# Seven rows normalised on GpSimd by adding the negated mean, with other planner margins and planner rules

## The chip, the cores and the metric

The kernel runs on one core of one Trainium2 chip. The metric is device time in microseconds (us), the median of the runs shown; lower is better. The core has five instruction streams that run side by side and wait for each other through semaphores: TensorE (PE, matmuls; PEld is its weight load), ScalarE (ACT), VectorE (DVE), GpSimd (POOL) and SyncE (SP, which only issues DMAs here). GpSimd issues DMAs too.

## What is computed

One token block of 2048 rows and 640 columns is normalised, and goes through an attention branch and a feed-forward branch, whose results are added to the input:

```
xn  = (x - mean(x)) / sqrt(var(x) + 1e-5)              # by row
q   = xn @ wq   (32 heads of 20);  k = xn @ wk;  v = xn @ wv   (one key/value head for all)
p   = softmax(q k^T / sqrt(20));   attn = (p v) @ wo
ffn = relu(xn @ w1 + b1)**2 @ w2 + b2
out = x + attn + ffn
```

All arrays are bf16, F is 1536. The scores are 32 heads x 2048 queries x 2048 keys.

## The kernel before: its stages and what orders them

**Tiles.** The rows are 16 tiles of 128 (`st` 0 to 15). Attention is 32 blocks: a block is 512 queries of four heads. In a block, each of 16 key tiles (`kt`, 128 keys) and each of the four heads is one score tile of 128 x 512: 2048 score tiles in all.

**Two ways to the exponential.** A score tile comes from one matmul, `ps<-qT,kT` (L426). 1396 of the 2048 tiles go to ACT, which evaluates exp on two PSUM banks at a time (L1007, 128x1024) into `PT`; PE then multiplies `PT` with the values `vx`. The other 652 tiles go in sets of four through an approximation: DVE turns the score into an integer that is read as a bf16 power of two (L1196, "D1"), then three more copies shifted by fixed steps are made on GpSimd (INT64_ADD, L1216) or DVE (L1218), and PE multiplies the copies with `vx` or the scaled `vxs`. Two copies of a set can first be added, either by a DMA that accumulates (issued on GpSimd, L1231, a "pair sum") or on DVE (L1236); that saves PE one multiplication per sum.

**Head of the kernel.** For every row tile: mean and variance (DVE `bn_stats`, L494 to L496; rows 2 and 4 on ACT, L489 and L490, which give the negated mean), 1/sqrt (rows 0 to 3 on ACT; the others on GpSimd as a power of -1/2, L505, "PW"), the normalisation "XN" at L507, five PE transposes (L618, "T"), a copy out of PSUM on DVE (L621, "TE"), and for each pair of rows the keys (L633). XN is `(x op mean) * rstd` in one `tensor_scalar`. Rows 7, 8, 9, 10, 11, 14 and 15 (`POOLXN`) do it on GpSimd, the others on DVE. `op` is subtract; rows 2 and 4, whose mean comes negated, use add. After the last XN, GpSimd loads another library ("LIB", L515), and only then can it run INT64_ADD.

**The planner.** The Python code that builds the kernel holds a list scheduler. Each operation has a planned duration, a priority and predecessors; latencies between engines stand in `LATS`; a DMA's planned landing is `lat`. The scheduler walks through a planned time and fixes, once and for all, the order of the instructions on each engine. On the chip each engine then runs its list strictly in that order and waits where a semaphore says so. Planned costs that matter here: XN on GpSimd 0.87, XN on DVE 0.36, PW 0.52, an INT64_ADD pass `PPASS` 1.015, the library 10.8. Margins: `DMARG` is added to the planned landing of DMAs of the softmax sums, `DMEND` takes its place for block 29 (the last that goes through those DMAs, `emit_norm`). `RULES` gives, for each 10 us of planned time ("stage"), weights and thresholds that decide which ready operation is taken first, when PE makes extra DVE tiles, when pair sums are made by DMA, and so on. `fill` matmuls (`ps<-kT,zeros`) are put where PE would idle in the head.

**End of a block and tail.** A block's sums go PSUM -> `OR` (DVE, L1075) -> DRAM -> `R` -> reciprocal (DVE, L1079) -> DRAM -> broadcast -> multiply (DVE, L1101, "CM"). Blocks 30 and 31 use transposes instead. In the tail PE multiplies the last quarter of the attention output with `wo`, DVE and ACT add and copy it, SP stores it.

Of the kernel before, what the change touches and what calls it, by code (L numbers as in the profile page):

```python
# [78 lines left out]
ADPL = 0.31  # L79
ADLEAD = 2.3  # L80
# [29 lines left out]
         11: {'BEHIND': 0.05, 'ADP': 5, 'ND': 1},  # L110
         12: {'BEHIND': 0.6, 'NOPEN': 4, 'JIT': 0.7},
         14: {'EVP': 0.3, 'DGAP': 1.5, 'DRATE': 0.95, 'BEHIND': 0.12, 'IDLE': 0.15, 'NOPEN': 3, 'EPS': 0.06, 'MRG': 2, 'M1': 0, 'ADP': 3.5, 'JIT': 0.7, 'PVA': 0.9, 'D1P': 0.3, 'SQP': 2, 'DQP': 0.5, 'KEEP': 2, 'ADDM': 0.6, 'ADPM': 2.4, 'KEEPM': 1, 'KEEPX': -1, 'DVL': 0.9, 'P2': 2},
         15: {'EVP': 0.3, 'DGAP': 1.5, 'DRATE': 0.95, 'BEHIND': 0.12, 'IDLE': 0.15, 'NOPEN': 3, 'EPS': 0.06, 'MRG': 2, 'M1': 0, 'ADP': 3.5, 'JIT': 1.3, 'PVA': 1.05, 'D1P': 0.3, 'SQP': 2, 'DQP': 0.5, 'KEEP': 2, 'ADDM': 0.6, 'ADPM': 2.4, 'KEEPM': 1, 'KEEPX': -1, 'DVL': 0.9, 'P2': 2},
         16: {'BEHIND': 0.05, 'IDLE': 0.15, 'EPS': 0.12, 'MRG': 1, 'JIT': 0.9, 'R3': 2, 'ND': 1, 'ADPM': 2.4},
         17: {'BEHIND': 0.05, 'IDLE': 0.15, 'EPS': 0.12, 'MRG': 1, 'JIT': 0.9, 'R3': 2, 'ND': 1, 'ADPM': 2.4},
         18: {'DGAP': 1.5, 'EPS': 0.06},
         19: {'EPS': 0.12},
         20: {'IDLE': 0.15, 'PP': 0.9},
         21: {'EVP': 1.1, 'IDLE': 0.15, 'JIT': 0.8, 'D1P': 0.5, 'PP': 0.9},
         22: {'EVP': 0.3, 'MPRIO': 0.9, 'DGAP': 0.8, 'DLAST': 6, 'DRATE': 0.95, 'BEHIND': 0.12, 'IDLE': 0.3, 'EPS': 0.06, 'MRG': 1, 'M1T': 1.2, 'JIT': 0.8, 'PVA': 0.9, 'ND': 1, 'KEEP': 0, 'KEEPM': 2, 'KEEPX': -1, 'DVL': 99},  # L120
# [26 lines left out]
         50: {'DVL': 0.9},
         51: {'EVP': 0.3, 'DVL': 0.9},
         52: {'EVP': 0.3, 'M1': 1, 'PVA': 0.9, 'DVL': 0.9},
         53: {'EPS': 0.03, 'JIT': 1.3, 'P2': 1},  # L150
         54: {'EVP': 0.8, 'DRATE': 0.95, 'URG': 4, 'M1T': 0, 'ADP': 3.5, 'JIT': 0.7, 'PVA': 0.9, 'D1P': 0.5, 'SQP': 3, 'ND': 2, 'KEEPM': 2},
         55: {'EVP': 0.8, 'DRATE': 0.95, 'URG': 9, 'EPS': 0.03, 'M1T': 0, 'ADP': 3.5, 'JIT': 0.7, 'PVA': 0.9, 'D1P': 0.5, 'SQP': 3, 'ND': 2, 'KEEPM': 2},
# [1493 lines left out]
```

## Time and profile before

| what | us |
|---|---|
| median of 3 runs (lowest, highest) | 678.58 (677.88, 679.56) |
| the profiled execution's own time | 677.92 |
| its span, first to last instruction | 676.1 |
| busy: PE / ACT / DVE / POOL | 663.3 / 653.1 / 606.6 / 588.3 |

The profile is one execution recorded by the hardware. "Busy" is the time in which an engine had an instruction in flight; the rest of the span it waited. The profile's other views are: windows (busy time of every engine in a stretch), waits (who waited for whom, total us, times, longest), the timeline of one engine (start, us, instruction; in brackets the idle time before it and what ended it), the instructions of one line (duration minimum/median/maximum in ns) and the chain that ended last.

### The profile page before, as it was taken

What the parts mean: (1) busy time and instruction counts of PE and PEld (TensorE: products, weight loads), DVE (VectorE), ACT (ScalarE), POOL (GpSimd) and SP (SyncE); (2) the same over time, 40 slices, a digit from 0 to 9 for tenths busy, and PEclk for the clock granted to TensorE, in tenths of its full rate; (3) what the DMA queues carried; (4) which work ended last, traced back from release to release, by engine and by line L of the source; (5) the groups of instructions that cost most, each with busy time, mean ns of one, the idle gap of its engine ahead of it and who ended that gap; (6) DMA issues with size and microseconds to landing.
All of it is one profiled execution on the core that took longest, in us unless ns stands there. A gap on an engine that the chain in (4) does not pass through costs nothing.

```text
span 676.1 us, 22515 instructions
## 1 busy us (share of the span) xinstructions
PE 663.3 (98%) x9617; PEld 212.5 (31%) x9618; DVE 606.6 (90%) x1069; ACT 653.1 (97%) x723; POOL 588.3 (87%) x591
## 2 busy tenths in 40 slices
PE   8789999999999999999999999999999999999998
PEld 4342222333332222233333322222333333222454
DVE  8669999999999999999999999999999999998654
ACT  7689999999999999999999999999999999999996
POOL 1947999999999989999999999999998999999331
PEclk9799999999999999999999999999999999999999
DMA  9496856686887755767786689575799878775744
GB/s 316 139 205 192 187 124 123 140 169 136 178 176 148 149 114 116 151 128 156 149 163 143 127 170 193 104 140 118 143 186 191 165 152 160 137 141 106 164 100 108
DMA packets 55278, 103.18 MB, mean 153 GB/s; under 512 B 17026, under 2 KB 33170, under 8 KB 55114
## 3 DMA queue, kind: packets, MB, share of 16 engines
q0 software_dynamic: 19088, 69.74, 55.3%
q1 hardware_dynamic: 35514, 31.63, 16.3%
q8 instruction: 75, 1.23, 0.7%
q10 hardware_dynamic: 576, 0.38, 0.2%
q14 instruction: 25, 0.20, 0.1%
HBM read 22.81 MB, written 9.69 MB: 48 GB/s over the span
## 4 chain that ended last, share of the span: by engine, by line
PE 57%; ACT 32%; POOL 4%; DMA 3%; DVE 2%; SPq 1%; issue 0%
PE ps L426 55%; ACT PT L1007 32%; POOL big L507 2%; DMA tmore<-tmore 1%; DMA tmore<-x_sb 1%; POOL tmore L1216 1%; POOL x_sb L1216 1%; PE ps L589 1%; SPq L1090 1%; SPq L1088 1%; DVE tmore L1196 1%; POOL rstd L505 0%; PE ps L618 0%; DVE big L507 0%; DMA R<-drs 0%
## 5 line engine op out<-in xcount | busy, mean ns | idle before, releaser
L1007 ACT ACTIVATE PT<-ps 128x1024 bf16<-128x1024 f32 x700 | 644.1, 1085 | 12.2 <-PE ps L426 11.5
L1196 DVE TENSOR_SCALAR tmore<-ps 128x512 uint16<-128x512 f32 x652 | 421.9, 684 | 32.6 <-PE ps L426 24.9
L1216 POOL INT64_ADD tmore<-tmore x217 | 240.6, 1200 | 38.0 <-DVE tmore L1196 18.6
L426 PE MATMUL ps<-qT,kT 20*128 20x512 bf16 x2048 | 265.0, 385 | 1.6 <-DVE tmore L1196 0.8
L1216 POOL INT64_ADD x_sb<-tmore x221 | 245.4, 1208 | 12.3 <-PE ps L426 3.4
L426 PEld LDWEIGHTS ps<-qT,kT 20*128 20x128 bf16 x2048 | 66.6, 91 | 255.0 <-ACT PT L1007 219.5
L426 PE MATMUL ps<-PT,vx 128*32 128x512 bf16 x1396 | 132.9, 388 | 0.0
L426 PE MATMUL ps<-xnT,w_sb 128*32 128x512 bf16 x960 | 77.5, 383 | 0.1
L426 PE MATMUL ps<-w_sb,big 128*32 128x320 bf16 x1536 | 74.7, 301 | 0.0
L1231 POOL DMA_DIRECT2D tmore<-tmore x63 | 64.6, 1035 | 3.0 <-POOL tmore L1216 3.0
L1231 POOL DMA_DIRECT2D x_sb<-tmore x61 | 65.1, 1074 | 2.1 <-POOL x_sb L1216 1.8
L426 PE MATMUL ps<-tmore,vxs 128*32 128x512 bf16 x636 | 57.5, 383 | 1.2 <-POOL tmore L1216 0.7
L426 PE MATMUL ps<-x_sb,vxs 128*32 128x512 bf16 x632 | 56.8, 383 | 0.1
L426 PEld LDWEIGHTS ps<-PT,vx 128*32 128x32 bf16 x1396 | 33.6, 93 | 63.3 <-issue 56.0
L426 PE MATMUL ps<-tmore,vx 128*32 128x512 bf16 x492 | 46.6, 382 | 0.0
L426 PEld LDWEIGHTS ps<-w_sb,big 128*32 128x32 bf16 x1536 | 34.0, 96 | 27.0 <-issue 17.7
L737 DVE TENSOR_SCALAR hT_tmp<-ps,b1col 128x512 bf16<-128x512 f32 x48 | 35.7, 744 | 3.2 <-PE ps L426 2.6
L426 PE MATMUL ps<-xnT,wq_sb 128*32 128x512 bf16 (+2 forms) x480 | 33.7, 356 | 0.0
L426 PE MATMUL ps<-x_sb,vx 128*32 128x512 bf16 x324 | 31.7, 383 | 0.0
L426 PE MATMUL ps<-wo_c,OC 128*32 128x320 bf16 x608 | 30.6, 301 | 0.0
L426 PEld LDWEIGHTS ps<-xnT,w_sb 128*32 128x32 bf16 x960 | 18.8, 95 | 24.9 <-issue 18.8
L745 DVE TENSOR_TENSOR big<-hT_tmp 128x512 bf16<-128x512 bf16 x48 | 24.8, 526 | 0.1
(95 smaller groups left out, 328.8 us busy)
## 6 DMA issues: line engine op xcount, KB each, us to landing
tmore<-tmore POOLq DMA_DIRECT2D x63, 512.0 KB, 5.4
x_sb<-tmore POOLq DMA_DIRECT2D x61, 512.0 KB, 5.5
w_sb<-in_B_w_dram SPq DMA_DIRECT2D x8, 480.0 KB, 10.1
big<-OR SPq DMA_DIRECT2D x71, 40.0 KB
big<-drs SPq DMA_DIRECT2D x71, 40.0 KB
xb<-in_A_x_dram SPq DMA_DIRECT2D x1, 2560.0 KB, 11.7
xb<-b2r POOLq DMA_DIRECT2D x1, 2560.0 KB, 18.7
xr<-xb SPq DMA_DIRECT2D x16, 160.0 KB, 3.9
```

The source lines that it names most:

```text
L426: return lambda e: e.matmul(out_, l, r, start=start, stop=stop, tile_position=tp, skip_group_check=loose)
L507: xn_op[st] = op(f"XN{st}", eng, dur, lambda e: e.tensor_scalar(out=xn_sb[:, st, :], in0=x_sb[:, st, :], scalar1=mv[:, st, 0:1], scalar2=r ...
L589: return [lambda e: e.matmul(ps[:, PVB, :], ones_bf[:, :], hT_tmp[:, 0, :], start=True, stop=True)]
L737: o = Op(f"RL{qc}_{f}", "DVE", 0.66, [lambda e: e.tensor_scalar(out=hT_tmp[:, k % 2, :], in0=ps[:, bk, :], scalar1=b1col[:, f:f + 1], scal ...
L745: q = op(f"SQ{qc}_{f}", "DVE", 0.34, lambda e: e.tensor_tensor(out=h2T[:, f, :], in0=hT_tmp[:, k % 2, :], in1=hT_tmp[:, k % 2, :], op=ALU. ...
L1007: return Op(f"ACT{st_['j']}", "ACT", ACB + ACM * n, [lambda e: e.activation(out=PT[:, s0:s0 + n, :], in_=ps[:, b0:b0 + (n - 1) * db + 1:db ...
L1088: dd = op(f"OM{b}_{j}", "SP", 0.76, lambda e, p0=p0, n=n, sl=sl, j=j, o0=o0: e.dma_start(cbuf(2 * sl)[p0:p0 + n, :], OR[32 * j + o0:32 * j ...
L1090: bc = op(f"BC{b}_{j}", "SP", 0.40, lambda e, p0=p0, n=n, sl=sl, j=j: e.dma_start(cbuf(2 * sl + 1)[p0:p0 + n, :], drs[b, 1][512 * j:512 * ...
L1196: d1 = op(f"D1_{n}_{i}", "DVE", 0.60, lambda e: e.tensor_scalar(out=L[:, cs].bitcast(U16), in0=ps[:, bank, :], scalar1=XA, scalar2=XB, op0 ...
L1216: fn = lambda e, T=T, j=j: e.int64_add(out=T.bitcast(I64), in0=L.bitcast(I64), in1=TSTEP * j * 0x0001000100010001)
L1231: p = op(f"AD{a}_{n}", "POOL", ADDUR, lambda e, src=src, dst=dst: e.dma_start(dst, src, accum_op=ALU.add), dp + [ad_last.get(k)], dma=adse ...
```

## The change

In the statistics of a row, rows in `POOLXN` get one more DVE operation "NM" that multiplies the mean by -1 in place, and their XN uses add. The planner adds `ADM` (0.5) to the planned landing of a pair sum where the instruction that waits for it is neither on PE nor itself a pair sum. `DMEND` goes from 1.0 to 2.5. `RULES` is replaced as a whole: other values in nearly every stage, some stages left to the defaults. Nothing else in the code changes.

```diff
-DMEND = 1.0
+DMEND = 2.5
...
+ADM = 0.5
...
 RULES = {0: {'WARM': 1},
-         1: {'EVP': 0.3, 'PBIAS': 5, 'DGAP': 1.5, 'DRATE': 0.95, 'BEHIND': 0.12, 'IDLE': 0.15, 'NOPEN': 3, 'EPS': 0.06, 'MRG': 1, 'M1': 0, 'ADP': 3.5, 'JIT': 0.7, 'PVA': 0.9, 'D1P': 0.3, 'PP': 4, 'SQP': 2, 'DQP': 0.5, 'KEEP': 2, 'ADDM': 1.5, 'ADPM': 2.4, 'KEEPM': 1, 'KEEPX': -1, 'DVL': 0.9, 'P2': 2, 'WARM': 1},
...
+         1: {'EVP': 0.3, 'DGAP': 0.8, 'DLAST': 6, 'DRATE': 0.95, 'BEHIND': 0.12, 'IDLE': 0.3, 'URG': 2, 'EPS': 0.06, 'MRG': 1, 'M1T': 1.2, 'JIT': 0.8, 'PVA': 0.9, 'ND': 2, 'KEEP': 0, 'KEEPM': 2, 'KEEPX': -1, 'DVL': 99, 'WARM': 1},
...
-            t = max(t, d.fin + (d.lat if d.lat is not None else ADPL if self.add and d.eng == "POOL" else LATS.get((d.eng, self.eng), 0.1)))
+            t = max(t, d.fin + (d.lat + (ADM if d.add and not self.add and self.eng != "PE" else 0.0) if d.lat is not None else ADPL if self.add and d.eng == "POOL" else LATS.get((d.eng, self.eng), 0.1)))
...
                 opm = ALU.subtract
+                if st in POOLXN:
+                    s1 = op(f"NM{st}", "DVE", 0.08, lambda e: e.tensor_scalar(out=mv[:, st, 0:1], in0=mv[:, st, 0:1], scalar1=-1.0, scalar2=None, op0=ALU.mult), [ag], prio=p - 0.1)
+                    opm = ALU.add
```

What the two built programs hold, counted in their instruction lists:

| instructions | before | after |
|---|---|---|
| ACT exp: pairs / singles / triples of tiles | 696 / 4 / 0 | 693 / 1 / 3 |
| score tiles on ACT / on DVE | 1396 / 652 | 1396 / 652 |
| INT64_ADD passes on POOL / passes on DVE | 438 / 51 | 437 / 52 |
| pair sums by DMA / on DVE | 128 / 3 | 133 / 0 |
| multiplications with the copies (`vx`, `vxs`) on PE | 2084 | 2076 |
| fill matmuls `ps<-kT,zeros` | 60 | 44 |
| NM on DVE | 0 | 7 |
| GpSimd's list up to the library load (PW, XN, one DMA) | same order | same order |

Beyond the head, the interleaving of the same kinds of work differs almost everywhere on PE, DVE and POOL. Near the end, the multiply "CM" of block 29 stands after block 30's transposes in DVE's list, where it stood before it.

More of the change, by code (lines that the diff above doesn't have):

```diff
@@ L110 @@
[L110 to L120, printed above, removed]
@@ L147 @@
[L147 to L152, printed above, removed]
-         56: {'DGAP': 0, 'DRATE': 0.95, 'IDLE': 0.15, 'URG': 6, 'ADP': 2, 'R3': 3, 'D1P': 0.3, 'PP': 0.9, 'KEEP': 0, 'ADPM': 2.4, 'DVL': 2.4},
@@ new lines @@
+         5: {'EVP': 0.3, 'DGAP': 0.8, 'DLAST': 6, 'DRATE': 0.95, 'BEHIND': 0.12, 'URG': 2, 'EPS': 0.06, 'MRG': 1, 'M1T': 1.2, 'JIT': 0.8, 'PVA': 0.9, 'ND': 2, 'KEEP': 0, 'ADDM': 0.6, 'ADPM': 3.5, 'KEEPM': 2, 'KEEPX': -1, 'DVL': 99, 'WARM': 1},
+         6: {'DRATE': 0.95, 'IDLE': 0.15, 'URG': 4, 'ADP': 2, 'D1P': 0.3, 'PP': 4, 'SQP': 0.7, 'KEEP': 0, 'ADPM': 2.4, 'DVL': 2.4},
+         7: {'EPS': 0.12, 'MRG': 1, 'R3': 2},
+         8: {'EVP': 0.3, 'DGAP': 0.8, 'DLAST': 6, 'DRATE': 0.95, 'BEHIND': 0.12, 'IDLE': 0.3, 'URG': 3, 'NOPEN': 4, 'EPS': 0.06, 'MRG': 1, 'M1T': 1.2, 'JIT': 0.8, 'PVA': 0.9, 'ND': 2, 'KEEPM': 2, 'KEEPX': -1, 'DVL': 99},
@@ new lines @@
+         10: {'EVP': 0.3, 'DGAP': 0.8, 'DLAST': 6, 'DRATE': 0.95, 'BEHIND': 0.12, 'IDLE': 0.15, 'URG': 2, 'EPS': 0.06, 'MRG': 1, 'M1T': 1.2, 'JIT': 0.8, 'PVA': 0.9, 'PVD': 0.9, 'ND': 2, 'KEEP': 0, 'ADDM': 0.7, 'KEEPM': 2, 'KEEPX': -1, 'DVL': 99},
+         11: {'EVP': 0.3, 'DGAP': 0.8, 'DLAST': 6, 'DRATE': 0.95, 'IDLE': 0.15, 'URG': 2, 'EPS': 0.06, 'MRG': 1, 'M1T': 1.2, 'JIT': 0.8, 'PVA': 0.9, 'PVD': 0.9, 'ND': 2, 'KEEP': 0, 'ADDM': 0.9, 'KEEPM': 2, 'KEEPX': -1, 'DVL': 99},
+         12: {'EPS': 0.12, 'MRG': 1, 'JIT': 0.9, 'R3': 2, 'PVA': 0.9},
@@ new lines @@
+         13: {'EVP': 0.8, 'DGAP': 0.8, 'DLAST': 6, 'DRATE': 0.95, 'BEHIND': 0.12, 'IDLE': 0.3, 'EPS': 0.06, 'MRG': 1, 'M1T': 1.2, 'JIT': 0.8, 'PVA': 1.05, 'ND': 2, 'KEEP': 0, 'KEEPM': 2, 'KEEPX': -1, 'DVL': 0.9},
+         14: {'EVP': 0.3, 'DGAP': 0.8, 'DLAST': 6, 'DRATE': 0.95, 'BEHIND': 0.12, 'IDLE': 0.3, 'EPS': 0.06, 'MRG': 1, 'M1T': 1.2, 'JIT': 0.8, 'PVA': 0.9, 'ND': 2, 'KEEP': 0, 'KEEPM': 2, 'KEEPX': -1, 'DVL': 99},
+         15: {'EVP': 0.8, 'DRATE': 0.95, 'IDLE': 0.15, 'URG': 4, 'M1T': 1.2, 'ADP': 3.5, 'JIT': 0.7, 'PVA': 0.9, 'D1P': 0.5, 'SQP': 3, 'ND': 2, 'KEEPM': 2, 'KEEPX': 1},
@@ new lines @@
+         17: {'DGAP': 1.5, 'JIT': 0.9, 'ADDM': 0.5},
+         18: {'DGAP': 0.8, 'DLAST': 2, 'NOPEN': 4, 'JIT': 0.7, 'D1P': 0.5, 'ND': 1, 'KEEP': 0, 'KEEPM': 1},
+         19: {'EPS': 0.06, 'M1T': 0, 'D1P': 0.5},
+         20: {'MPRIO': 0.3, 'ADDM': 1.2, 'P2': 1},
+         21: {'MPRIO': 0.3, 'MRG': 9, 'ADDB': 0, 'JIT': 1.1, 'ADDM': 1.2, 'P2': 1},
+         22: {'EVP': 0.3, 'DGAP': 1.5, 'DRATE': 0.95, 'BEHIND': 0.12, 'IDLE': 0.15, 'NOPEN': 3, 'EPS': 0.03, 'MRG': 1, 'M1': 0, 'ADP': 3.5, 'JIT': 0.8, 'PVA': 0.9, 'D1P': 0.3, 'PP': 4, 'SQP': 2, 'DQP': 0.5, 'KEEP': 2, 'ADDM': 0.6, 'ADPM': 2.4, 'KEEPM': 1, 'KEEPX': -1, 'DVL': 0.9, 'P2': 2},
@@ new lines @@
+         23: {'DLAST': 2, 'MRG': 2, 'PVA': 1, 'KEEP': 3},
+         24: {'EVP': 0.3, 'DGAP': 0.8, 'DLAST': 6, 'DRATE': 0.95, 'BEHIND': 0.12, 'IDLE': 0.15, 'URG': 2, 'EPS': 0.06, 'MRG': 1, 'M1T': 1.2, 'JIT': 0.8, 'PVA': 0.9, 'PVD': 0.9, 'ND': 2, 'KEEP': 0, 'ADDM': 0.7, 'KEEPM': 2, 'KEEPX': -1, 'DVL': 99},
+         25: {'DRATE': 0.8, 'SQP': 3},
+         26: {'EVP': 0.8, 'DGAP': 0.8, 'DLAST': 6, 'DRATE': 0.95, 'BEHIND': 0.12, 'IDLE': 0.3, 'EPS': 0.06, 'MRG': 1, 'M1T': 1.2, 'JIT': 0.8, 'PVA': 1.05, 'ND': 2, 'KEEP': 0, 'KEEPM': 2, 'KEEPX': -1, 'DVL': 0.9},
@@ new lines @@
+         28: {'MPRIO': 0.3, 'PVA': 1.05, 'ADDM': 1.2, 'P2': 1},
+         30: {'PBIAS': 8, 'NOPEN': 3},
+         31: {'PBIAS': 8, 'NOPEN': 3},
+         32: {'EVP': 0.3, 'DGAP': 0.8, 'DLAST': 6, 'DRATE': 0.95, 'BEHIND': 0.12, 'IDLE': 0.3, 'EPS': 0.06, 'MRG': 1, 'M1T': 1.2, 'JIT': 0.8, 'PVA': 0.9, 'ND': 2, 'KEEP': 0, 'ADDM': 1.5, 'KEEPX': -1, 'DVL': 99},
+         33: {'PBIAS': 8, 'M1T': 1.2},
+         34: {'EVP': 0.3, 'DGAP': 0.8, 'DLAST': 6, 'DRATE': 0.8, 'BEHIND': 0.12, 'IDLE': 0.3, 'EPS': 0.03, 'MRG': 1, 'M1T': 1.2, 'ADP': 5, 'JIT': 0.8, 'R3': 2, 'PVA': 0.9, 'PVD': 1.5, 'D1P': 3, 'KEEP': 0, 'ADDM': 0.3, 'KEEPM': 2, 'KEEPX': 0, 'DVL': 99},
@@ new lines @@
+         35: {'EPS': 0.03, 'KEEP': 2},
+         36: {'EPS': 0.03, 'PVA': 0.8, 'KEEP': 2},
+         37: {'DLAST': 2, 'EPS': 0.03, 'PVA': 0.8, 'PP': 0.9, 'KEEP': 2, 'DVL': 99},
+         38: {'M1T': 0.6, 'D1P': 0.5},
+         39: {'EVP': 0.8, 'PBIAS': 8, 'DRATE': 0.95, 'URG': 9, 'M1T': 1.2, 'ADP': 3.5, 'JIT': 0.8, 'PVA': 1, 'ND': 2, 'KEEPM': 0, 'KEEPX': 1},
+         40: {'EVP': 0.8, 'PBIAS': 8, 'MPRIO': 0.3, 'DGAP': 0.8, 'DLAST': 6, 'DRATE': 0.95, 'BEHIND': 0.12, 'IDLE': 0.3, 'NOPEN': 4, 'EPS': 0.06, 'MRG': 2, 'M1T': 1.2, 'JIT': 1.1, 'PVA': 0.8, 'PVD': 1.2, 'DQP': 1.5, 'ND': 1, 'KEEPM': 2, 'KEEPX': -1, 'DVL': 99},
@@ new lines @@
+         41: {'EVP': 0.8, 'PBIAS': 8, 'MPRIO': 0.5, 'DRATE': 0.95, 'IDLE': 0.6, 'URG': 4, 'M1T': 1.2, 'ADP': 3.5, 'JIT': 1.1, 'PVA': 0.9, 'D1P': 0.5, 'SQP': 3, 'ND': 2, 'KEEPX': 1},
+         43: {'DGAP': 0.3, 'IDLE': 0.3, 'URG': 4, 'R3': 3, 'QKP': 0, 'ND': 1, 'KEEPX': 2},
+         44: {'URG': 6, 'EPS': 0.12, 'MRG': 1, 'R3': 2},
+         45: {'IDLE': 0.3, 'URG': 4, 'PVA': 0.8, 'PVD': 1.2, 'PP': 4, 'ND': 1, 'ADDM': 0, 'KEEPX': 2},
+         46: {'NOPEN': 4, 'EPS': 0.12, 'D1P': 1},
+         47: {'DGAP': 0.3, 'IDLE': 0.3, 'URG': 4, 'QKP': 0, 'ND': 1, 'KEEPX': 2},
@@ new lines @@
+         48: {'PBIAS': 8, 'DGAP': 0.3, 'IDLE': 0.3, 'URG': 4, 'DQP': 1.5, 'QKP': 0, 'ND': 1, 'KEEPX': 2},
+         49: {'IDLE': 0.15, 'URG': 4, 'DQP': 3, 'ND': 1, 'KEEPX': 2, 'P2': 1},
+         50: {'EVP': 0.3, 'PBIAS': 5, 'MPRIO': 0.9, 'DGAP': 1.5, 'DRATE': 0.95, 'BEHIND': 0.12, 'IDLE': 0.15, 'NOPEN': 3, 'EPS': 0.06, 'MRG': 1, 'M1': 0, 'ADP': 3.5, 'JIT': 0.7, 'R3': 1, 'PVA': 0.9, 'D1P': 0.3, 'SQP': 2, 'DQP': 3, 'KEEP': 0, 'ADDM': 1, 'ADPM': 2.4, 'KEEPM': 1, 'KEEPX': 0, 'DVL': 0.9, 'P2': 2},
@@ new lines @@
+         51: {'EVP': 0.3, 'PBIAS': 5, 'MPRIO': 0.9, 'DGAP': 0.5, 'DRATE': 0.95, 'BEHIND': 0.12, 'IDLE': 0.15, 'NOPEN': 3, 'EPS': 0.06, 'MRG': 1, 'M1': 0, 'M1T': 0.9, 'ADP': 3.5, 'JIT': 0.7, 'R3': 1, 'PVA': 0.9, 'D1P': 0.3, 'SQP': 2, 'DQP': 3, 'KEEP': 0, 'ADDM': 1, 'ADPM': 2.4, 'KEEPM': 1, 'KEEPX': 0, 'DVL': 0.9, 'P2': 2},
+         52: {'EVP': 1.1, 'URG': 3, 'EPS': 0.06},
+         53: {'DRATE': 0.95, 'NOPEN': 3, 'MRG': 1, 'D1P': 0.3},
+         54: {'EVP': 0.8, 'DGAP': 0.8, 'DLAST': 6, 'DRATE': 0.95, 'BEHIND': 0.12, 'IDLE': 0.3, 'EPS': 0.06, 'MRG': 1, 'M1T': 1.2, 'JIT': 0.8, 'PVA': 1.05, 'ND': 2, 'KEEP': 0, 'KEEPM': 2, 'KEEPX': -1, 'DVL': 0.9},
@@ new lines @@
+         55: {'PBIAS': 8, 'EPS': 0.12, 'MRG': 1, 'R3': 2},
+         56: {'MPRIO': 0.3, 'ADDM': 1.2, 'P2': 1},
+         57: {'MPRIO': 0.3, 'ND': 1, 'ADDM': 1.2, 'P2': 1},
+         58: {'MPRIO': 0.3, 'ND': 1, 'ADDM': 1.2, 'P2': 1},
+         59: {'EVP': 0.8, 'PBIAS': 8, 'DRATE': 0.95, 'URG': 9, 'M1T': 1.2, 'ADP': 3.5, 'JIT': 0.8, 'PVA': 1, 'QKP': 0, 'ND': 2, 'KEEPM': 0, 'KEEPX': 1},
+         60: {'EVP': 0.8, 'PBIAS': 8, 'DRATE': 0.95, 'URG': 9, 'EPS': 0.06, 'M1T': 1.2, 'ADP': 3.5, 'JIT': 0.8, 'PVA': 1, 'ND': 2, 'KEEPM': 0, 'KEEPX': 1, 'DVL': 1.8},
@@ new lines @@
+         61: {'PBIAS': 8, 'NOPEN': 3, 'M1T': 0.6},
+         62: {'EVP': 0.3, 'DGAP': 1.5, 'DRATE': 0.95, 'BEHIND': 0.12, 'IDLE': 0.15, 'NOPEN': 3, 'EPS': 0.06, 'MRG': 0, 'M1': 0, 'ADP': 3.5, 'JIT': 0.7, 'PVA': 0.9, 'D1P': 0.3, 'PP': 0.9, 'SQP': 2, 'DQP': 0.5, 'QKP': 0, 'KEEP': 2, 'ADPM': 2.4, 'KEEPM': 1, 'KEEPX': -1, 'DVL': 0.9, 'P2': 2},
+         63: {'EVP': 0.3, 'MPRIO': 1.2, 'DGAP': 1.5, 'DRATE': 0.95, 'BEHIND': 0.12, 'IDLE': 0.15, 'NOPEN': 3, 'EPS': 0.06, 'MRG': 0, 'M1': 0, 'ADP': 3.5, 'JIT': 0.7, 'PVA': 0.9, 'D1P': 0.3, 'PP': 0.9, 'SQP': 2, 'DQP': 0.5, 'QKP': 0, 'KEEP': 2, 'ADPM': 2.4, 'KEEPM': 1, 'KEEPX': -1, 'DVL': 0.9, 'P2': 1},
@@ L164 @@
+         64: {'DGAP': 0.5, 'IDLE': 0.3, 'URG': 4, 'NOPEN': 1, 'MRG': 0, 'ADDN': 0.2, 'QKP': 0, 'ND': 1, 'KEEPM': 0, 'KEEPX': 2, 'DVL': 0.9},
+         65: {'DGAP': 0.8, 'IDLE': 0.3, 'URG': 4, 'NOPEN': 1, 'MRG': 0, 'ADDN': 0.2, 'R3': 1, 'QKP': 0, 'ND': 1, 'KEEP': 0, 'KEEPM': 0, 'KEEPX': 2, 'DVL': 0.9},
+         66: {'DGAP': 0.8, 'IDLE': 0.3, 'URG': 4, 'NOPEN': 1, 'MRG': 0, 'ADDN': 0.2, 'R3': 1, 'QKP': 0, 'ND': 1, 'KEEP': 0, 'KEEPM': 0, 'KEEPX': 2, 'DVL': 0.9}}
 HOOK = None
```

48 lines of the change are left out of this document (3 added, 45 removed).

## The prediction

> **What bounds the kernel now.** I read the windows first: which engine never rests, and where.
>
> ```profile
> 11.77:47.79 36.02, 30.43 (x474) 14.44 (x474) 25.00 (x78) 26.37 (x28) 25.86 (x20) 0.91 0.77 210
> ...
> sum 400.00, PE 399.34 PEld 117.16 DVE 377.57 ACT 400.00 POOL 386.49; mean PE 99.83 PEld 29.29 DVE 94.39 ACT 100.00 POOL 96.62
> ```
>
> The first row is the head, from the first exp to the keys of the last rows (length, then busy PE, PEld, DVE, ACT, POOL; granted clock; DMA). The second sums four windows from 100 to 500 us. There ACT is busy all 400 us. PE shows 99.83%, but it waits for ACT, as the waits of the whole span say, and so does its weight load:
>
> ```profile
> PEld ps L426 <- ACT PT L1007: 223.6, 574, 0.5
> ...
> ACT PT L1007 <- PE ps L426: 11.5, 11, 3.1
> ```
>
> So the score tiles on ACT set the pace from about 50 us on: 437 exps took 401.2 us there, 0.918 each.
>
> ```profile
> L1007 ACT ACTIVATE PT<-ps 128x1024 bf16<-128x1024 f32 x437 | 401.2, 1106 | 0.0
> ```
>
> The chain that ended last says 57% PE and 32% ACT; between engines that feed each other without a gap it may follow either, so I don't read a bound from it. The time to be won is ACT's idle time. ACT's waits, first for 11.77 to 75 us, then for 75 to 668 us, and its timeline, say where it lies:
>
> ```profile
> ACT PT L1007 <- PE ps L426: 9.8, 8, 3.1
> ```
> ```profile
> ACT PT L1007 <- PE ps L426: 1.7, 3, 1.2
> ```
> ```profile
> 21.30 5.09 ACT L1007 ACTIVATE PT<-ps 128x1024 bf16<-128x1024 f32 x5 [1.40 <-PE ps L426]
> 29.46 1.94 ACT L1007 ACTIVATE PT<-ps 128x1024 bf16<-128x1024 f32 x2 [3.07 <-PE ps L426]
> 32.82 1.02 ACT L1007 ACTIVATE PT<-ps 128x1024 bf16<-128x1024 f32 x1 [1.43 <-PE ps L426]
> ...
> 44.67 12.02 ACT L1007 ACTIVATE PT<-ps 128x1024 bf16<-128x1024 f32 x13 [3.12 <-PE ps L426]
> ```
>
> Four gaps, 1.40 + 3.07 + 1.43 + 3.12 = 9.0 us of the 9.8. What did PE and DVE wait for there?
>
> ```profile
> PE ps L618 <- POOL big L507: 5.2, 4, 1.8
> ...
> DVE xnT L621 <- PE ps L618: 6.3, 7, 2.0
> ```
> ```profile
> L507 DVE TENSOR_SCALAR big<-x_sb,mv,rstd x9: 433/440/668, 7.1 to 36.2; 128x640 bf16<-128x640 bf16 x9
> L507 POOL TENSOR_SCALAR big<-x_sb,mv,rstd x7: 2501/2504/2528, 17.9 to 40.9; 128x640 bf16<-128x640 bf16 x7
> ```
> ```profile
> L505 POOL TENSOR_TENSOR rstd<-mv,nhalf x12: 547/558/687, 12.1 to 40.3; 128x1 f32<-128x1 f32 x12
> ```
>
> PE waits for XN on GpSimd before its transposes, DVE for the transposes, ACT for PE. XN takes 2.50 us there, always. A row on GpSimd costs 0.56 (PW) + 2.50 + 0.08 in gaps = 3.14 us, and a new key tile gives ACT four score tiles, two exps, 2 x 0.918 = 1.84 us. While rows come every 3.14 us, ACT starves.
>
> **The change part by part.** *XN with add.* Seven instructions. The trace shows no such add on GpSimd, so I bound it: not below 0.56 (PW on one element), not above 2.50 (the subtract), since nothing in the form is larger. Between them lies a rate that GpSimd does show:
>
> ```profile
> 54.13 5.09 POOL L1216 INT64_ADD tmore<-tmore  x5 [10.68 <-DVE OR L1075]
> ```
>
> 1.02 us for 512 elements of 64 bits, 2.0 ns each, would make 640 elements 1.28 us. The planner carries 0.87 for XN on GpSimd; its other costs stand within 0.04 of their rows (PW 0.52 against 0.56, a pass 1.015 against 1.02), only XN is off by three. Whether 0.87 was once right for an add is not shown. I take 0.9, from between the pass's rate and PW, and keep both ends. What decides is whether a row falls below ACT's 1.84 us: the add must cost less than 1.84 - 0.56 - 0.08 = 1.20. At 0.9 it does; at 1.28 five consecutive rows (7 to 11) lose 5 x 0.08 = 0.4 us; at 2.50 nothing is won.
>
> The subtract alone is 2.50 us for 640 elements, 3.9 ns each. [...]
>
> *What is late next in the head.* With XN short, the head's 36.02 us window cannot shrink below its busiest engine: ACT 26.37, DVE 25.00 plus seven NMs, nearest row the 152 ns of the epsilon add:
>
> ```profile
> L499 DVE TENSOR_SCALAR mv<-mv 128x1 f32<-128x1 f32 x11 | 1.7, 152 | 0.3
> ```
>
> 7 x 0.152 = 1.06, so DVE 26.06. The limit of the gain is 36.02 - 26.37 = 9.65 us. Two engines almost equally full, each waiting for the other through PE, don't reach it. How near? The part of the head that the first XN on GpSimd (17.88 us) hardly touches shows it:
>
> ```profile
> 11.77:20.41 8.64, 6.97 (x116) 3.37 (x116) 7.39 (x25) 7.86 (x8) 4.75 (x6) 1.00 1.03 384
> 20.41:29.82 9.41, 7.23 (x105) 3.31 (x109) 5.90 (x19) 5.26 (x6) 9.10 (x7) 0.81 0.50 153
> 29.82:38.30 8.48, 8.48 (x132) 3.79 (x128) 6.29 (x20) 6.87 (x8) 6.96 (x8) 0.81 0.48 100
> ```
>
> ACT 7.86 of 8.64, 91%, against 56% and 81% in the next two. At 91% the head takes 26.37 / 0.91 = 29.0 us: **7.0 us less**. NM itself lies beside PW, 0.56 us, for which XN waits anyway; without that cover it would cost 0.15 a row. [...]
>
> *The library and GpSimd's first pass.* The load starts at the last XN's end and its end opens the passes; POOL's timeline:
>
> ```profile
> 40.95 2.50 POOL L507 TENSOR_SCALAR big<-x_sb,mv,rstd 128x640 bf16<-128x640 bf16 x1
> ```
>
> The 10.68 us that POOL idles before the passes (row above) stay (the releaser named is only the last semaphore; it is the load). They start earlier by at least as much as the head shrinks, so passes come no later against the rest. Cost 0.
>
> *The new order from 50 us on.* ACT has the same 1396 tiles; three exps fewer, three of them triples, moves ACT by well under 0.5 us, taken as 0. On DVE three sums go (below), one pass comes; on POOL one pass goes, five sum issues of about 1.05 come; PE loses two groups of four multiplications. All lies beside ACT, which is full for those 400 us, and costs nothing; if that cover went, the five issues would be 5.3 us of GpSimd.
>
> ```profile
> L1236 DVE TENSOR_TENSOR tmore<-tmore,x_sb 128x2048 bf16<-128x2048 bf16 x1 | 1.7, 1675 | 0.0
> ...
> L1236 DVE TENSOR_TENSOR tmore<-tmore 128x2048 bf16<-128x2048 bf16 x1 | 1.2, 1221 | 0.0
> L1236 DVE TENSOR_TENSOR x_sb<-x_sb,tmore 128x2048 bf16<-128x2048 bf16 x1 | 1.2, 1165 | 0.0
> ```
>
> *The margins.* They can win the 1.7 us that ACT idles after 75 us, no more. The largest piece is block 29's reciprocal, for which DVE waited and after which ACT did:
>
> ```profile
> 632.70 0.25 DVE L1079 RECIPROCAL R<-R 128x16 f32<-128x16 f32 x1 [1.88 <-DMA R<-drs]
> ```
> ```profile
> 635.04 15.41 ACT L1007 ACTIVATE PT<-ps 128x1024 bf16<-128x1024 f32 x17 [1.16 <-PE ps L426]
> ```
>
> DVE's new list has more tiles ahead of that reciprocal, so the wait should go; a new order brings other small ones. Bounds +2 to -1.7; I take **-0.5**. Moving CM of block 29 behind block 30's transposes only delays matmuls that PE also has later.
>
> *Sum.* Span 676.1 - 7.0 - 0.5 = 668.6. The profiled execution took 677.92, 1.82 above its span: 670.4. The median, 678.58, is 0.66 above that execution: 671.1, said as **671**.
>
> **The rivals.** A measurement of this kernel can tell about 0.3% from no change: 2.0 us.
>
> *A, the forecast:* add below 1.20 us, 667 to 673.5. For it: the four gaps all end with XN. Against: DVE nearly as full as ACT.
>
> *B, the add costs what the subtract costs* (the change doesn't do what it says). The head stays, NM adds at most 1.06 on a DVE that waits 6.3 us there: 678.6 - 0.5 + 0.5 = 678.6, 677 to 680. For it: DVE shows one price for both forms (rows 2 and 4 add; minimum and median 433 and 440). [...]
>
> *C, half the gain:* the add at about 1.7, or DVE's statistics the bound at 85% for ACT: 26.37 / 0.85 = 31.0, gain 5.0, less a new order's 1 us of waits: 674.6, 673.5 to 676.6.
>
> *D, slower: pair sums that land late.* PE multiplies a sum's result and its buffer is reused, so a late one holds PE's list and then ACT. The chain of before has such a piece, and a sum's median landing is 5.4 us:
>
> ```profile
> 516.59 8.48 DMA tmore<-tmore
> ```
> ```profile
> tmore<-tmore POOLq DMA_DIRECT2D x63, 512.0 KB, 5.4
> ```
>
> Before, three stalls cost ACT 1.7 us together, 0.57 each. It decides once ACT loses more than 7.5 + 2.0 = 9.5 us, 17 such stalls among 133 sums. At 20: 20 x 0.57 = 11.4, 671.1 + 11.4 = 682.5. For it: five more sums, the whole order new, DMA shares near 0.75. Against: 128 sums made at most three.
>
> **How the numbers follow.** A 0.74, B 0.10, C 0.08, D 0.08. The time is A's. Range 667.0 (all 9.65 us and the 1.7 would give 667.2) to 676.6 (C's end, with the add's price up to about 1.7): it holds A and C, 0.82, and leaves out B and D. Faster by over 0.3% (below 676.5): A and C, 0.82. Within: B but for a fifth, 0.08. Slower: D and that fifth, 0.10.
>
> **What would show it.** XN on GpSimd about 0.9 us in the row of its line; ACT's waits in the head at 2 to 3 us instead of 9.8; the first INT64_ADD at 44 to 47 us instead of 54.13; the granted clock near 1.00 all through the head; ACT full from 100 to 500 us; the first exp at 11.8 and the last exp about 7.5 us earlier than before. Wrong if XN stays near 2.50 (B), if ACT's waits between 75 us and the last exp exceed 4 us (D), or if DVE is over 95% busy in the head with ACT still waiting (C).

## The result, and the profile after

The changed kernel takes 669.66 us, the median of 6 runs (668.91 to 671.50), against 678.43 for the kernel before beside it: ratio 0.9873, interval [0.9855, 0.9892], 8.8 us less. Some executions of these kernels run at a lower granted clock and longer (in `add_only` 728.25 us at 0.962 beside 708.02 at 0.993); the medians given here are of all executions, the ratios compare the others alone, which are two of six in `add_only` and three of six in `old_rules`. Repeated later, beside another set of runs of the kernel before, the changed kernel gave 0.9881 [0.9845, 0.9918]. The profiled execution took 671.5 us, 1.84 above the median, so its span shows less of the gain (676.1 to 669.7) than the medians do.

First the price in question, the instructions of XN's line and of NM's line in the changed kernel (nanoseconds minimum/median/maximum; for NM busy us, mean ns and idle us before it):

```profile
L508 DVE TENSOR_SCALAR big<-x_sb,mv,rstd x9: 430/441/790, 7.3 to 31.2; 128x640 bf16<-128x640 bf16 x9
L508 POOL TENSOR_SCALAR big<-x_sb,mv,rstd x7: 870/874/880, 17.9 to 32.6; 128x640 bf16<-128x640 bf16 x7
```
```profile
L500 DVE TENSOR_SCALAR mv<-mv 128x1 f32<-128x1 f32 x7 | 1.0, 144 | 0.0
```

XN on GpSimd is 0.874 us where it was 2.504. The windows of the head, as before, and two of the stretch behind it:

```profile
11.77:20.41 8.64, 8.39 (x128) 4.06 (x125) 8.09 (x32) 8.56 (x11) 3.79 (x7) 1.00 1.07 385
20.41:29.82 9.41, 9.41 (x182) 5.16 (x180) 9.15 (x36) 9.30 (x11) 7.47 (x10) 1.00 0.73 201
29.82:38.30 8.48, 8.48 (x148) 4.50 (x146) 6.39 (x22) 7.29 (x9) 3.22 (x5) 1.00 1.03 181
...
100.00:200.00 100.00, 100.00 (x1445) 30.19 (x1437) 94.33 (x157) 100.00 (x111) 97.66 (x100) 1.00 0.79 161
...
300.00:400.00 100.00, 99.92 (x1413) 30.06 (x1405) 91.67 (x149) 99.58 (x110) 96.06 (x98) 1.00 0.77 154
```

The fourth busy figure is ACT: 8.56, 9.30 and 7.29 us where 7.86, 5.26 and 6.87 stood. The granted clock is 1.00 in all three (1.00, 0.81, 0.81 before). Next comes ACT's timeline from its first exp; of the four gaps that made up 9.0 us, one of 1.19 is left:

```profile
12.24 22.54 ACT L1008 ACTIVATE PT<-ps 128x1024 bf16<-128x1024 f32 x24
35.97 12.02 ACT L1008 ACTIVATE PT<-ps 128x1024 bf16<-128x1024 f32 x13 [1.19 <-PE ps L424]
48.47 25.97 ACT L1008 ACTIVATE PT<-ps 128x1024 bf16<-128x1024 f32 x28 [0.48 <-PE ps L424]
75.09 5.77 ACT L1008 ACTIVATE PT<-ps 128x1024 bf16<-128x1024 f32 x6 [0.65 <-PE ps L424]
```

And where the profiled time went, from ACT's whole list and its end (groups of exps by shape, with count, busy us, mean ns, and idle us before them; then the timeline of the end), first before:

```profile
L1007 ACT ACTIVATE PT<-ps 128x1024 bf16<-128x1024 f32 x696 | 642.5, 1087 | 12.2 <-PE ps L426 11.5
L1007 ACT ACTIVATE PT<-ps 128x512 bf16<-128x512 f32 x4 | 2.5, 628 | 0.0
```
```profile
635.04 32.97 ACT L1007 ACTIVATE PT<-ps 128x1024 bf16<-128x1024 f32 x37 [1.16 <-PE ps L426]
```

Then the same in the changed kernel:

```profile
L1008 ACT ACTIVATE PT<-ps 128x1024 bf16<-128x1024 f32 x693 | 638.4, 1091 | 5.0 <-PE ps L424 4.6
L1008 ACT ACTIVATE PT<-ps 128x1536 bf16<-128x1536 f32 x3 | 4.4, 1463 | 0.0
L1008 ACT ACTIVATE PT<-ps 128x512 bf16<-128x512 f32 x1 | 0.7, 653 | 0.0
```
```profile
599.52 60.33 ACT L1008 ACTIVATE PT<-ps 128x1024 bf16<-128x1024 f32 x64
663.59 1.25 ACT L1297 ACTIVATE out_sb<-ps 128x320 bf16<-128x320 f32 x3 [3.73 <-PE ps L424]
```

ACT's idle time among the exps went from 12.2 to 5.0 us (-7.2), the exps' busy time from 645.0 to 643.5 (-1.5), and the first exp starts 0.47 later. So the last exp ends at 599.52 + 60.33 = 659.85 instead of 635.04 + 32.97 = 668.0, 8.15 earlier. The tail from there to the end of the span grew from 8.1 to 9.85 us (+1.75), which leaves the -6.4 of the two profiled spans.

### The profile page after: what moved, and what is told of

The parts are those of the page before. It is cut to its first block, busy times and chain, and to the rows that moved or that the text cites. A ratio compares the mean times of both kernels' runs of the same rounds, so it can differ in the third digit from the quotient of the medians.

```text
span 669.7 us, 22479 instructions
## 1 busy us (share of the span) xinstructions
PE 661.3 (99%) x9591; PEld 212.2 (32%) x9592; DVE 604.2 (90%) x1074; ACT 651.9 (97%) x720; POOL 580.7 (87%) x595
## 4 chain that ended last, share of the span: by engine, by line
PE 63%; ACT 19%; DMA 7%; POOL 5%; DVE 3%; issue 1%; SPq 1%; POOLq 0%
PE ps L424 62%; ACT PT L1008 19%; POOL x_sb L1217 3%; DMA tmore<-tmore 2%; POOL tmore L1217 2%; DMA x_sb<-tmore 2%; DVE tmore L1197 1%; DMA x_sb<-x_sb 1%; DMA x_sb<-in_A_x_dram 1%; DMA R<-drs 1%; PE ps L619 1%; POOL x_sb L1232 0%; DVE x_sb L1219 0%; SPq L719 0%; DVE big L746 0%
## 5 line engine op out<-in xcount | busy, mean ns | idle before, releaser
L1197 DVE TENSOR_SCALAR tmore<-ps 128x512 uint16<-128x512 f32 x652 | 421.7, 683 | 36.5 <-PE ps L424 30.4
L1217 POOL INT64_ADD x_sb<-tmore x219 | 246.9, 1255 | 30.0 <-DVE tmore L1197 19.8
L424 PE MATMUL ps<-qT,kT 20*128 20x512 bf16 x2048 | 268.2, 384 | 1.7 <-ACT PT L1008 1.0
L1217 POOL INT64_ADD tmore<-tmore x218 | 248.5, 1273 | 22.3 <-DVE OR L1076 12.1
L1232 POOL DMA_DIRECT2D tmore<-tmore x66 | 70.9, 1082 | 4.2 <-POOL tmore L1217 3.0
L1232 POOL DMA_DIRECT2D x_sb<-tmore x63 | 67.2, 1067 | 4.0 <-POOL x_sb L1217 2.2
L424 PE MATMUL ps<-tmore,vx 128*32 128x512 bf16 x468 | 44.5, 382 | 0.7 <-DMA tmore<-tmore 0.6
L826 DVE TENSOR_TENSOR out_sb<-ps,xr 128x320 bf16<-128x320 f32 x24 | 11.6, 484 | 13.2 <-PE ps L424 13.1
```

Of the source, the lines that this page charges most:

```text
L424: return lambda e: e.matmul(out_, l, r, start=start, stop=stop, tile_position=tp, skip_group_check=loose)
L826: o = Op(f"OE{n}", "DVE", 0.40, [lambda e: e.tensor_tensor(out=out_sb[:, slot, cs], in0=ps[:, bk, 0:HW], in1=xrow(st, cs), op=ALU.add)], [ ...
L1197: d1 = op(f"D1_{n}_{i}", "DVE", 0.60, lambda e: e.tensor_scalar(out=L[:, cs].bitcast(U16), in0=ps[:, bank, :], scalar1=XA, scalar2=XB, op0 ...
L1217: fn = lambda e, T=T, j=j: e.int64_add(out=T.bitcast(I64), in0=L.bitcast(I64), in1=TSTEP * j * 0x0001000100010001)
L1232: p = op(f"AD{a}_{n}", "POOL", ADDUR, lambda e, src=src, dst=dst: e.dma_start(dst, src, accum_op=ALU.add), dp + [ad_last.get(k)], dma=adse ...
```

## The experiments

I held theory P: the gain is the price of XN in the head, and the rest of the change is worth nothing. Its rival R: the new order and margins bring half or more. The obvious test is to take the change apart: one part alone, or one part left out.

**The add alone.**

```diff
 (the kernel before)
                 opm = ALU.subtract
+                if st in POOLXN:
+                    s1 = op(f"NM{st}", "DVE", 0.08, ...)
+                    opm = ALU.add
```

> The kernel before with nothing but the add: seven NM on VectorE and XN with add on GpSimd; old margins, old rules. Theory P (the price of XN in the head is all): XN about 0.87 us, ACT's waits before 75 us at 2 to 3 us instead of 9.8, time 7.0 to 8.8 us below before, 669.7 to 671.5. Theory R (the new order brings half or more of the gain): 674 or above.

Measured: a ratio to the kernel before of 1.0498 [1.0444, 1.0551], 5% slower.

**The add left out**, the same lines taken from the changed kernel.

> The changed kernel with the subtract put back and NM taken out; new margins, new rules. Theory P: XN 2.50 us, ACT idles 9 to 10 us in the head again, 677.5 to 679.5. Theory R: 674 or below.

Measured: 716.50 us, 1.0583 [1.0544, 1.0621].

**The margins left out.**

```diff
 (the changed kernel)
-DMEND = 2.5
+DMEND = 1.0
-ADM = 0.5
+ADM = 0.0
```

> The changed kernel with DMEND 1.0 and ADM 0, as before; add and new rules stay. Theory P: within 1 us of the changed kernel, 668.7 to 670.7. If the margins save waits for late sums and for the last reciprocals: 670.7 to 672, and ACT's waits after 75 us up by 1 to 2 us.

Measured: 703.74 us, 1.0372 [1.0355, 1.0389].

**The rules left out**: `RULES` of before in the changed kernel.

> The changed kernel with the rules of before; add and new margins stay. Theory P: within 2 us of the changed kernel, 668.7 to 671.7. Theory R: 674 or above. Rules that were searched for other margins may fit badly: then the loss must show as ACT's waits after 75 us, more than 3 us.

Measured: 1.0470 [1.0435, 1.0504].

All four are far slower than both kernels. P says 669 to 679 for each of them, and R cannot make both "add alone" and "add left out" lose. Only the expectation for `old_rules` had named what could happen, rules that fit badly, with ACT's waits after 75 us above 3 us as its sign, and it had named it for that part alone. The heads do follow the price: ACT's waits from 11.77 to 75 us are 2.3, 1.5 and 1.5 us in `add_only`, `old_margins` and `old_rules`, which add, and 11.7 in `no_add`, which subtracts. The loss lies behind: after 75 us ACT waits 30.6 us (`add_only`), 18.9, 23.2 and 19.8 us for PE. Those of `add_only` and `old_rules` come from executions with a mean granted clock of 0.975 and 0.967, so part of them may be the clock's. The profile of `old_margins`, with a clock of 0.997, shows more. Its score tiles on DVE (line, busy us, mean ns, idle before), its exps, and ACT's waits up to 75 us and after:

```profile
L1197 DVE TENSOR_SCALAR tmore<-ps 128x512 uint16<-128x512 f32 x620 | 402.8, 683 | 87.5 <-PE ps L424 79.5 <-DMA x_sb<-tmore 1.8 <-DMA tmore<-tmore 0.6
```
```profile
L1008 ACT ACTIVATE PT<-ps 128x1024 bf16<-128x1024 f32 x709 | 654.1, 1101 | 21.0 <-PE ps L424 20.4
```
```profile
ACT PT L1008 <- PE ps L424: 1.5, 2, 1.2
```
```profile
ACT PT L1008 <- PE ps L424: 18.9, 16, 4.7
```

The head is as good as the changed kernel's (1.5 us of waits). But DVE has 620 score tiles instead of 652, so ACT has 32 more, and after 75 us ACT waits 18.9 us; DVE's tiles wait 79.5 us for PE, where they waited 30.4 in the changed kernel. A tile on DVE takes 683 ns in both. ACT's exps are busy 659.8 us instead of 643.5 and idle 21.0 instead of 5.0: 16.3 + 16.0 us, which accounts for the 32.2 by which the two profiled spans differ. Hence a third theory, F: a set of rules belongs to one plan. One more planned operation of 0.08 us, or 0.5 us on a latency, shifts the planned times; what follows is another order, in which the values chosen stage by stage no longer meet the states that they were chosen for. Taking a part out of the change then measures a plan without fitting rules, not the part. To test P, the order must stay and only the price change.

**The order of before, XN by add.** The negation is put into the planned operation that adds epsilon, so the planner sees nothing new.

```diff
 (the kernel before)
                 opm = ALU.subtract
+                if st in POOLXN:
+                    ve.parts.append(lambda e: e.tensor_scalar(out=mv[:, st, 0:1], in0=mv[:, st, 0:1], scalar1=-1.0, scalar2=None, op0=ALU.mult))
+                    opm = ALU.add
```

> The kernel before with XN by add and nothing else moved: the planner is not told; each negation follows the epsilon add inside the same planned operation, so rules, margins and the order of all other instructions are those of before. Theory P (the price of XN on the chip is the gain): 7 to 9 us below before, 669.5 to 671.5, ACT's waits before 75 us at 1 to 3 us. Theory R (the new order and margins bring half or more): 674 or above.

Measured: 670.37 us, 0.9895 [0.9863, 0.9926]. In its head, ACT is busy 34.17 us of the window in which it was busy 26.37 (the first row; the others are two of the stretch behind it):

```profile
11.77:47.79 36.02, 35.34 (x578) 16.07 (x579) 31.65 (x98) 34.17 (x38) 18.38 (x24) 1.00 0.95 247
```
```profile
47.79:60.00 12.21, 11.11 (x118) 2.49 (x114) 8.61 (x15) 9.84 (x12) 9.64 (x11) 0.79 0.85 200
60.00:75.00 15.00, 15.00 (x116) 2.52 (x108) 9.18 (x16) 10.16 (x10) 7.54 (x8) 0.50 0.59 145
```

The profiled execution took 682.59 us, 12.2 above the median. Up to 47.79 us the granted clock is 1.00 and ACT waits 1.6 us, but from 47.79 to 75 us the clock is 0.79 and 0.50 and ACT waits another 7.2. So the 1 to 3 us that were expected up to 75 us were 8.8 here, and only the head can be read from this profile; for the rest the times speak.

**The order of the changed kernel, XN by subtract.** NM stays and multiplies by +1.

```diff
 (the changed kernel)
-  ... scalar1=-1.0, scalar2=None, op0=ALU.mult), [ag], prio=p - 0.1)
-                    opm = ALU.add
+  ... scalar1=1.0, scalar2=None, op0=ALU.mult), [ag], prio=p - 0.1)
+                    opm = ALU.subtract
```

> The changed kernel with NM multiplying by +1 and XN subtracting: every engine's list is instruction for instruction that of the changed kernel, only XN costs 2.50 us again. Theory P: 677 to 679.5, ACT's waits before 75 us about 10 us. Theory R: 674 or below. By the doubled XN (3.0 us for 0.87 us a row) the threshold of 1.20 us would give 3.0 x (2.50 - 1.20) / (1.75 - 1.20) = 7.1 us: 676.8.

Measured: 677.91 us, 0.9999 [0.9967, 1.0031]: the whole gain is gone, with every instruction of the changed kernel in its place. Its XN, ACT's waits (11.77 to 75 us) and its pairs of exps:

```profile
L508 POOL TENSOR_SCALAR big<-x_sb,mv,rstd x7: 2502/2505/2528, 18.2 to 40.4; 128x640 bf16<-128x640 bf16 x7
```
```profile
ACT PT L1008 <- PE ps L424: 8.6, 7, 3.0
```
```profile
L1008 ACT ACTIVATE PT<-ps 128x1024 bf16<-128x1024 f32 x693 | 638.6, 1093 | 11.3 <-PE ps L424 10.9
```

These two settle P against R: the price alone moves either order by 7 to 8.5 us, and neither order is measurably better than the other at the same price. In two rows of the head the granted clock is low again, 0.73 from 20.41 to 29.82 us and 0.90 from there to 38.30, where the changed kernel has 1.00; so in both orders the clock was low there with the dear XN and 1.00 with the cheap one. What share of ACT's gaps comes from the lower clock rather than from the wait for XN itself was not separated.

**XN at twice the price.**

```diff
 (the changed kernel)
             xn_op[st] = op(f"XN{st}", ...)
+            if eng == "POOL":
+                xn_op[st].parts.insert(0, lambda e: e.tensor_scalar(out=junk, ...))   # junk: a part of out_sb or OC, not yet in use
```

> The changed kernel with each of the seven XN on GpSimd preceded by a copy of itself that writes to unused memory: 1.75 us a row for XN, order of everything else unchanged. Theory P with its threshold (an add over 1.20 us makes the rows slower than ACT's 1.84 us each): rows 7 to 11 and 14, 15 cost 2.4 us, 7 x 0.55 = 3.9 us at most, 672.5 to 673.5. Rival, every us on GpSimd costs the same: 8.8 us for 7 x 1.63 us is 0.77 per us, 7 x 0.87 x 0.77 = 4.7, 674.4. Rival, hidden in GpSimd's idle time in the head (9.0 us of waits for VectorE): 669 to 670.5.

Measured: 672.63 us, 0.9890 [0.9852, 0.9927]. The median is in P's range, 3.0 above the changed kernel. "Every us costs the same" (674.4, or 0.994) lies just outside the interval, "hidden" inside it, and the changed kernel was not run beside this one; so by the times alone the choice stays open. The kept profile is of an execution of 679.07 us, 6.4 above the median. ACT's gaps up to 42 us in it, and two rows of its windows:

```profile
14.57 2.85 ACT L1012 ACTIVATE PT<-ps 128x1024 bf16<-128x1024 f32 x3 [0.27 <-PE ps L424]
18.54 1.02 ACT L1012 ACTIVATE PT<-ps 128x1024 bf16<-128x1024 f32 x1 [1.11 <-PE ps L424]
19.71 6.77 ACT L1012 ACTIVATE PT<-ps 128x1024 bf16<-128x1024 f32 x7 [0.16 <-PE ps L424]
27.60 3.98 ACT L1012 ACTIVATE PT<-ps 128x1024 bf16<-128x1024 f32 x4 [1.12 <-PE ps L424]
32.30 6.67 ACT L1012 ACTIVATE PT<-ps 128x1024 bf16<-128x1024 f32 x7 [0.71 <-PE ps L424]
40.47 12.02 ACT L1012 ACTIVATE PT<-ps 128x1024 bf16<-128x1024 f32 x13 [1.51 <-PE ps L424]
```
```profile
11.77:20.41 8.64, 8.39 (x113) 3.73 (x110) 6.65 (x26) 7.11 (x9) 3.94 (x6) 0.80 1.03 383
...
47.79:60.00 12.21, 10.58 (x100) 2.05 (x92) 7.53 (x13) 8.56 (x10) 8.26 (x9) 0.72 0.60 180
```

The gaps are 4.9 us together, against 1.2 in the changed kernel, but the first three lie where the granted clock is 0.80. The last three, 3.3 us, lie where it is 1.00; they speak against "hidden". Another 5.3 us of waits follow between 52 and 64 us, where the clock is low again, so this execution doesn't give the size for the median. In the medians the first 0.87 us on top cost 3.0 us over seven rows, the next 0.75 (to 2.50) 5.3. That is how a threshold would look, but a straight line would give 4.4 for the first part, and the interval is 2.5 us to either side: the threshold of 1.20 us is not shown.

**The forms by themselves.**

```diff
 (a kernel of its own; REP is 3, n is 640 or 320)
+            for r in range(REP):
+                for t, n, o0, o1 in ((t_sub_mul, 640, ALU.subtract, ALU.mult), ...   # and seven other forms
+                    ...
+                        e.tensor_scalar(out=t[:, r, :], in0=x_sb[:, 0:n], scalar1=sc[:, 0:1], scalar2=sc[:, 1:2], op0=o0, op1=o1)...
```

> Not the kernel: eight forms of tensor_scalar on GpSimd alone, 128 x 640 bf16, three times each, nothing beside them (the output is only a copy of the input). If subtract as such is slow: every form with a subtract 2.4 to 2.5 us, in whichever place, every form without one 0.8 to 0.9. If only subtract in first place is slow: multiply-then-subtract 0.87. If it is a price by element: half the width 1.3 to 1.4 us for subtract-multiply and 0.5 to 0.6 for add-multiply; if a fixed cost: 2.0 us or more for half the width. [...]

Measured (groups of GpSimd; the mean in ns is the figure before the last bar; a name starting with `h_` has 320 columns):

```profile
L58 POOL TENSOR_SCALAR t_mul_sub<-x_sb,sc 128x640 bf16<-128x640 bf16 x3 | 7.5, 2509 | 0.0
L58 POOL TENSOR_SCALAR t_sub_mul<-x_sb,sc 128x640 bf16<-128x640 bf16 x3 | 7.5, 2498 | 2.8 <-DMA x_sb<-in_A_x_dram 2.8
L56 POOL TENSOR_SCALAR t_sub<-x_sb,sc 128x640 bf16<-128x640 bf16 x3 | 5.7, 1885 | 0.0
L56 POOL TENSOR_SCALAR t_add<-x_sb,sc 128x640 bf16<-128x640 bf16 x3 | 5.6, 1882 | 0.0
L58 POOL TENSOR_SCALAR h_sub_mul<-x_sb,sc 128x320 bf16<-128x320 bf16 x3 | 4.3, 1437 | 0.0
L58 POOL TENSOR_SCALAR t_mul_add<-x_sb,sc 128x640 bf16<-128x640 bf16 x3 | 2.6, 875 | 0.0
L58 POOL TENSOR_SCALAR t_add_mul<-x_sb,sc 128x640 bf16<-128x640 bf16 x3 | 2.6, 874 | 0.0
L58 POOL TENSOR_SCALAR h_add_mul<-x_sb,sc 128x320 bf16<-128x320 bf16 x3 | 1.8, 602 | 0.0
```

With nothing beside it the subtract still takes 2.50, so no neighbour made the price. It is one by element: (2498 - 1437) / 320 = 3.3 ns with a subtract, (874 - 602) / 320 = 0.85 ns for add and multiply, over 0.33 to 0.38 us that a straight line through the two widths leaves. The place of the operation makes no difference on 640 columns (2498 and 2509, 874 and 875 ns). One expectation fell: an add alone is as slow as a subtract alone, 1.88 us. So a subtract isn't the only dear form; of those measured, the pair of an add and a multiply is the cheap one.

**The margins left out, rules fitted anew**, to test F: 21 of the stages get other rules, each taken, apart from the entry `WARM`, from those that stand in either kernel.

```diff
 (the changed kernel with DMEND = 1.0 and ADM = 0.0)
 RULES = {0: {'WARM': 1},
...   # 21 stages with other rules
```

> The changed kernel with DMEND 1.0 and ADM 0 as before, and the rules of 21 stages chosen anew for that plan, each from the rules that stand in either kernel. The plan holds 1412 tiles on ACT and 636 on VectorE (changed kernel 1396 and 652; old_margins with the rules as they were 1428 and 620). If what old_margins lost (34 us) was the fit of rules to plan: most of it comes back, and 16 tiles more on ACT than the changed kernel cost 16 x 0.459 = 7.3 us: 677 to 682. If it was the margins themselves, waits for late sums: still over 695, with ACT's waits after 75 us near the 18.9 of old_margins.

Measured: 681.87 us, 1.0055 [1.0020, 1.0090]; DVE has 636 score tiles:

```profile
L1198 DVE TENSOR_SCALAR tmore<-ps 128x512 uint16<-128x512 f32 x636 | 411.6, 683 | 58.6 <-PE ps L425 49.0 <-POOL x_sb L1218 1.7 <-DMA x_sb<-tmore 1.3
```

22 of the 34 us come back by the choice of rules alone, and ACT's waits after 75 us fall from 18.9 to 6.4 us. That speaks for F in this part; in the other three F was not tested. What is left fits the tiles: 16 more on ACT than in the changed kernel are 7.3 us, and ACT's waits after 75 us are 4.1 us longer than in its repeat below (6.4 against 2.3), together 11.4 of 11 to 12. The fit of the rules stopped short of the changed kernel's, so whether the margins themselves are worth anything stays open.

**The changed kernel again**, beside the kernel with refitted rules.

> The changed kernel once more, on the same chip as old_margins_refit: 668.5 to 671.5.

Measured: 671.05 us, 0.9881 [0.9845, 0.9918]. None of the kernels tried here is faster than the changed one.

## Why the prediction was right, point by point

- **The bound.** Shown: with the order of the changed kernel, taking the price away from seven instructions of the head cuts ACT's waits up to 75 us from 8.6 to 1.7 us, 6.9 less, and the last exp ends 6.6 us earlier (666.4 to 659.85). After the head ACT is 99.6 to 100% busy in the windows shown, before and after. PE, the busiest engine of the head before with 30.43 us, was not the limit of the gain: 6.1 us of it are the fills (the row below), which leaves 24.3, less than ACT's 26.37.

```profile
L426 PE MATMUL ps<-kT,zeros 128*32 128x512 bf16 x60 | 6.1, 449 | 0.0
```

- **The add's price, taken as 0.9 between 0.56 and 2.50.** Measured 0.874. No row of the kernel before gave it, so that the choice came within 3% was partly luck. What pointed to it was that the planner's other costs agreed with their rows. The scaling of INT64_ADD (1.28) was too high by half, and the reading that the subtract alone makes the price was too narrow: an add without a multiply costs 1.88.
- **The head, -7.0.** ACT's waits up to 75 us fell from 9.8 to 1.7, 8.1 (to 2.2 in the repeat, 7.6). The 91% chosen for ACT was a little low: in the three windows of the changed kernel's head it is busy 25.15 of 26.53 us, 95%. DVE became as full as was foreseen, 23.63 of 26.53, 89% (26.06 of 29.0, 90%, by the forecast). In the second window it is 97% busy (9.15 of 9.41), yet ACT is 99% busy there, so DVE wasn't the bound that C feared. The granted clock, foreseen near 1.00, was 1.00; why it was 0.81 in two rows before is not shown: in the second of them PE is busy all 8.48 us.
- **NM at no cost.** Seven at 144 ns. With them in the list and XN at its old price the time is that of before (0.9999 [0.9967, 1.0031]), so any cost is below some 2 us. That PW hides them isn't shown beyond that.
- **The first pass at 44 to 47.** It came at 45.61. But the prediction put POOL's 10.68 us of idle time before it down to the load alone, and that was too much: with the order of before and the add, POOL idles only 9.50 us there. In the changed kernel it idles 12.09, and the releaser named, the copy of block sums on DVE, ends 0.23 us before the pass (in the repeat it is a score tile on DVE). So the load is no longer what the pass waits for, which the prediction hadn't said. A cost of it doesn't show.
- **The margins and the new order, -0.5: this term failed in its parts.** It was +2.95 in the profiled execution, outside its bounds of +2 to -1.7: ACT's waits after 75 us rose from 1.7 to 2.9 (2.3 in the repeat), and the tail grew by 1.75, which the prediction had put at nothing. The tail belongs to the order: it is 9.6 to 9.8 us in the repeat and in the changed order with subtract, and 8.1 in the order of before with the add. The wait of block 29's reciprocal is gone, as meant, and so is ACT's gap of 1.16 behind it. In its place came small ones: a reciprocal at 72.35 us waits 0.95, DVE's waits for pair sums went from 0.4 to 0.9, under the margin that was to spare them, and ACT has eight short waits after 75 us instead of three. Which part of the change makes which of these was not separated. In the medians the two orders are equal at equal price, within about 2 us.
- **The triples, taken as 0**: -1.5 us of exp time. It goes with the list and not with the gaps: with the changed list and the subtract the exps are busy 643.7 us though ACT idles 11.3 us between them, so 1.3 of the 1.5 us stay. The three triples at 1463 ns, against 1091 for a pair, and the three singles fewer are what differs in that list; their shares were not separated.
- **The sum came out partly by luck.** Of the profiled span, the head gave 8.1 instead of 7.0 and the exps 1.5 instead of 0; the margins and the new order took 2.95 instead of giving 0.5, and the first exp came 0.47 later. The errors nearly cancel: with rounding these make the 6.4 us of the profiled spans, where 7.5 was forecast.
- **The rivals.** B is excluded by the price, C by the add's price and by ACT's 95% in the head, D by ACT's waits after 75 us (2.9 us, not 11).
- **What was right by more luck than I knew.** The prediction costed the re-chosen rules at nothing because the amounts of work were equal in both lists. That held. But the same rules over an order one operation away cost 25 to 40 us, and no rival of the prediction says so: that the rules don't fit their plan. The counts in the built programs (652 score tiles on DVE in both) were what excluded it here, and they would have shown it: 596 to 620 in the four parts that failed.

## What to carry to other kernels

A price that is far from what a planner or a neighbour carries for the same instruction is worth a bench of its forms: rewriting the operation, here a subtract as an add of the negated value inside a two-operation instruction, made it 2.9 times as fast (2.50 to 0.87 us) at the price of one tiny instruction (144 ns on DVE). Where a scheduler orders the program, a change is tested by keeping the order and changing the price; leaving out a part makes another order, and then measures that. Compare the amounts of work on each engine in the built programs before reading anything from such a run.
